# Where the expert weights are split into high and low parts: GpSimd, or ScalarE and VectorE

## The chip, the core and the metric

One core of a Trainium2 chip runs the whole program. Time is the device time of one execution in microseconds (us). Five engines have an instruction queue each and run it in order: TensorE (PE: matmuls; PEld: its weight loads), VectorE (DVE), ScalarE (ACT), GpSimd (POOL) and SyncE (SP), which here only issues DMAs.

## The reference

```python
def reference(**kwargs):
    ...
    attn_out = _attn_ref(**attn_kwargs)      # 2 x 8 heads, 768 tokens, 64 wide, masked by LSH buckets
    x = attn_out.transpose(0, 2, 1, 3).reshape(1536, 512)
    x = ((x @ w1) * (x @ w2)) @ w3 @ w_out                      # 512 -> 1024 -> 1024 -> 512
    p = domain_probs / (domain_probs.sum(-1, keepdims=True) + 1e-09)
    for e in range(4):                                          # the experts
        out += p[:, e:e + 1] * (np.maximum(x @ w1_e, 0.0) @ w2_e)   # 512 -> 1024 -> 512
```

All is fp32. The change touches the second and third stage, the products with `w3 @ w_out` and the four experts.

## The kernel before

**Arithmetic.** A product of fp32 matrices is made of three matmuls in fp32r: high x high, high x low, low x high. So each operand is split: the high part is a copy into an fp32r tile (`hi_of` on ACT, `pool_hi` on GpSimd), the low part is the value less its high part (`lo_of` on DVE, `pool_lo` on GpSimd).

**Stages after attention.** (1) `A` and `B` are the products with w1 and w2; their element product g is kept. (2) `W` i (i = 0 to 7) is one eighth of w3 @ w_out, 24 matmuls each, and its result is split by ACT and DVE. (3) `H` blk, ff multiplies g by it: three blocks of 512 tokens with eight steps of 12 matmuls. The steps of block 0 are mixed among the W, those of block 1 and 2 follow. (4) For each expert, `M` and `N` are the first layer, by Strassen's seven products over two token blocks (M, 512 columns) and the third block (N, 256 columns), for four column pairs fp of the weight; `O` are the steps of the second layer, 24 matmuls per fp for block 0 (mixed among M and N), and 96 each for blocks 1 and 2 behind them. One fp has 7 x 6 matmuls M, 7 x 6 matmuls N and 24 matmuls O.

**Weights of the experts.** `conv_full` loads a quarter of a first layer (`load_u`, into buffer `wraw` 0) or of a second layer (`load_o`, `wraw` 1) by two DMAs of 256 KB and splits it on GpSimd: a first-layer quarter as two tiles of 128x256 (`dh`, and `dc`/`dd` for the low parts), a second-layer quarter as one tile of 128x1024 (`dh`, `dd`). For the first layer, DVE also makes five sums of its parts for Strassen's products (`z`, into `zf`, all reading `wraw`), ACT makes their high parts (`zh`, 128x1024 and 128x256) and DVE their low parts (`zl`); the split sums lie in one tile, which the next sums may take only when the N products 1, 2, 5, 7 and 6 have read it. `wraw` is loaded anew when its splits and its sums are done. The weights of stages 1 and 2 go through `conv64`, ten steps on ACT and DVE per half tile, which this change leaves as they are.

**Sums of the input.** At the end of H's block 1, DVE makes sums of the result (`xs`, L899), which ACT and DVE split (`yh`, `xd`); at the end of block 2, the sums `ys` (L875) and their splits `yi`, `yd`, which N reads. N's four results are combined by DVE (`ya1` to `y22`) in tiles called kept(2, ff), until block 2's O reads them.

**Order.** `op` records each step with an engine, a planned duration, the steps it waits for and a priority. `emit_all` plays the program by these durations and the delays in `LAT` (a DMA: its duration and 1900 ns more), takes on each engine the ready step of least priority value, and writes the instructions in the order that comes out. Planned durations decide the order alone; on the chip every engine goes through that order and waits where an operand is late.

Of the kernel before, what the change touches and what calls it, by code (L numbers as in the profile page):

```python
# [71 lines left out]
def tile_lsh_attention_moe(ctx, tc, qk, v, projc, w1, w2, w3T, w_out, dp, e1, e2, out):  # L72
# [107 lines left out]
    def conv64(n, dst, half, src):  # L180
        r = raws[n % NRAW]

        def hi_():
            return slots[dst][:, 0, half * 512:(half + 1) * 512]

        def lo_():
            return slots[dst][:, 1, half * 512:(half + 1) * 512]

        ri = r.bitcast(I32)
        lw, hw = (ri.rearrange("p (a b) -> p a b", b=2)[:, :, i] for i in range(2))  # L190
        c, t = cbuf[:, n % NCB, 0], cbuf[:, n % NCB, 1]
        beside = n < NBESIDE
        side, sdur, seng, minus = ("POOL", 1290, nc.gpsimd, pool_lo) if beside else ("DVE", 620, nc.vector, lo_of)
        slow = (400, 700) if beside else (335, 602)
        return [
            ("SP", 2700, [("cd", n - NRAW), ("c2", n - NRAW)], "cl",
             lambda: nc.sync.dma_start(out=ri.rearrange("p (a b) -> p a b", a=src.shape[1]), in_=src)),
            ("ACT", 570, [("cl", n), ("cq", n - NCB)], "ca",
             lambda: nc.scalar.activation(out=f(c), in_=f(hw), func=AF.Abs)),
            ("DVE", slow[0], [("ca", n)], "c0",  # L200
             lambda: nc.vector.tensor_scalar(out=f(c), in0=f(c), scalar1=EXP_LO, scalar2=EXP_HI, op0=ALU.max, op1=ALU.min)),
            ("DVE", slow[0], [("c0", n)], "c1",
             lambda: nc.vector.tensor_scalar(out=t, in0=c, scalar1=3, scalar2=0x3FFFFFFF, op0=ALU.logical_shift_left,
                                             op1=ALU.bitwise_and)),
            ("DVE", slow[1], [("c1", n)], "c2",
             lambda: nc.vector.scalar_tensor_tensor(out=c, in0=hw, scalar=-0x40000000, in1=t, op0=ALU.bitwise_and,
                                                    op1=ALU.bitwise_or)),
            ("DVE", slow[0], [("c2", n)], "c3",
             lambda: nc.vector.tensor_scalar(out=t, in0=c, scalar1=-0x800000, scalar2=None, op0=ALU.bitwise_and)),
            ("ACT", 520, [("c2", n)], "ch",  # L210
             lambda: nc.scalar.activation(out=hi_(), in_=f(c), func=AF.Copy)),
            (side, sdur, [("ch", n)], "cp", lambda: minus(lo_(), f(c), hi_())),
            ("DVE", slow[1], [("c3", n)], "cd",
             lambda: nc.vector.scalar_tensor_tensor(out=f(t), in0=lw.bitcast(U32), scalar=2.0 ** -52, in1=f(t),
                                                    op0=ALU.mult, op1=ALU.mult)),
            (side, sdur, [("cp", n), ("cd", n)], "cq",
             lambda: seng.tensor_tensor(out=lo_(), in0=f(lo_()), in1=f(t), op=ALU.add)),
        ]
# [425 lines left out]
    nh = [0]  # L644
# [88 lines left out]
    ZB = L_[0]  # L733
    raw_free = [[(k, 2 * (4 + 4 + 4 + KF) - NRAW + i) for k in ("cd", "c2")] for i in range(NRAW)]

    def conv_full(name, dst, fn, src, fp, after, raw, z_after=None):
        T = clock[0]
        r = raws[raw]
# [6 lines left out]
                out=r[:, half * 512:(half + 1) * 512].rearrange("p (a b) -> p a b", a=s_.shape[1]), in_=s_),  # L745
               raw_free[raw], T - 1.5 * P)
        if z_after is None:
            op(("dh", name), "POOL", 1170, lambda: pool_hi(slots[dst][:, 0], r), got + after, T)
            op(("dd", name), "POOL", 2420, lambda: pool_lo(slots[dst][:, 1], r, slots[dst][:, 0]), [("dh", name)], T)
        else:  # L750
            rq = r.rearrange("p (j k f c) -> p j f k c", j=2, k=2, f=2)
            for i in range(2):
                key = ("dd" if i else "dc", name)
                op(("dh", name, i), "POOL", 310, lambda i=i: pool_hi(a_at(fp, i)[:, 0], rq[:, i, i]), got + after, T)
                op(key, "POOL", 640, lambda i=i: pool_lo(a_at(fp, i)[:, 1], rq[:, i, i], a_at(fp, i)[:, 0]), [("dh", name, i)], T)
        raw_free[raw] = [("dd", name), ("dc", name)]
        if z_after is None:
            return
# [1 line left out]
        for m, (sa, a, b) in enumerate(((1.0, (0, 0), (1, 1)), (-1.0, (0, 1), (1, 1)), (-1.0, (0, 0), (1, 0)),  # L760
                                        (1.0, (1, 0), (1, 1)), (1.0, (0, 1), (0, 0)))):
            def go(m=m, sa=sa, a=a, b=b):
                nc.vector.scalar_tensor_tensor(out=zs_t[1][:, m], in0=q[:, a[0], a[1]], scalar=sa,
                                               in1=q[:, b[0], b[1]], op0=ALU.mult,
                                               op1=ALU.add if m == 0 else ALU.subtract)

            op(("z", name, m), "DVE", 340, go, got + z_after, T)
            raw_free[raw].append(("z", name, m))
        for i, (ms, dur) in enumerate(((slice(0, 4), 1080), (slice(4, 5), 270))):
            src = lambda ms=ms: zs_t[1][:, ms]  # L770
            op(("zh", name, i), "ACT", dur, lambda i=i, src=src: hi_of(zz(i)[:, 0], src()),
# [69 lines left out]
    for blk in range(NB):  # L841
        hb = u_ps if blk % 2 else o_ps
        for ff in range(KF):
# [61 lines left out]
    x_in = [("xd", m, k) for m in range(1, 8) for k in range(2)]  # L905
    y_in = [("yd", m) for m in range(1, 8)]
    u_in = [k for r in freed[1] for k in r]
    load_u(0, 1, [("W", KF - 1)], [("N", 0, 0, m) for m in (1, 2, 5, 6, 7)])
    last_o[0] = [("hl", NB - 1, d) for d in range(KM)]

    def kept(blk, ff):
        return G[ff // 4][:, ff % 4] if blk == 1 else G[2][:, ff] if ff < 4 else f(cbuf.rearrange(
            "p a b c -> p (a b) c"))[:, ff - 4]

    def relu_hi(n, key, after, m):
        op(key, "ACT", 480, lambda: nc.scalar.activation(out=hl_t[n % 2][:, 0], in_=m_t[m], func=AF.Relu), after, clock[0])  # L916
# [29 lines left out]
    def put_down(e, blk, ff, n, ready, ps, free_):  # L946
# [1 line left out]
        order[blk].append(ff)  # L948
        down(("O", e, blk, ff), n, lambda d, a: hl_t[n % 2][:, a, d * 128:(d + 1) * 128],
             lambda d, b: slots[OB[ff // 2]][:, b, (ff % 2) * 512:(ff % 2 + 1) * 512],  # L950
             i == 0, i == KF - 1, ready + [("dd", ("O", e, ff // 2))] + (free_ if i == 0 else [("O", e, blk, order[blk][-2])]), ps)

    kept_key = {}
    for e in range(NE):
        order = [[] for _ in range(NB)]
        old = x_in + y_in + [("gl", nh[0] - 1 - k) for k in range(16 if e else 0)]
        for fp in range(4):
            name = ("U", e, fp)

            def w(fp=fp):  # L960
# [146 lines left out]
```

## Time and profile before

| | us |
|---|---|
| median of 3 runs (994.08, 994.24, 997.37) | 994.24 |
| the profiled execution | 993.28 |
| its span, first to last instruction | 991.5 |

The span begins with attention (to about 264 us), then stage 1 (to 373), W with block 0 of H (to 439), the other blocks of H (to about 485, where the first M stands among them) and the experts, of which the second begins at 616.05, the third at 740.08 and the fourth at 864.14. The TensorE clock was granted at 0.999 of full speed on average. Busy time says only that an engine has an instruction under way; where the order of the queues decides, one reads what each engine waited for and which instruction took longer than its like.

### The profile page before, as it was taken

The page shows a single profiled execution, that of the slowest core. Times are in us where ns is not written, and L with a number is a line of the kernel's source. Part 1 is how long each engine was busy: PE and PEld are TensorE (multiplying, and loading weights), DVE is VectorE, ACT ScalarE, POOL GpSimd, SP SyncE. Part 2 cuts the span into 40 slices and gives each one's busy share as a digit, 9 for nine tenths or more (in the row PEclk, how much of TensorE's full clock was granted, in tenths as well). Part 3 has the DMA queues.
Part 4 walks back from the last instruction along what each step waited for, and adds up shares of the span by engine and source line. Part 5 has one row for each costly group of instructions (what it writes and reads, how often), then busy time and mean ns, then how long its engine had stood idle before and what let it go on. Part 6 is the DMA issues. An engine that isn't in the chain of part 4 may idle for free.

```text
span 991.5 us, 14182 instructions
## 1 busy us (share of the span) xinstructions
PE 970.0 (98%) x5227; PEld 832.6 (84%) x5227; DVE 718.1 (72%) x1341; ACT 428.6 (43%) x784; POOL 280.9 (28%) x319
## 2 busy tenths in 40 slices
PE   8999999999999999999889999999999999999998
PEld 7989899889788888877778888888888888888886
DVE  7999999999599975965886644766446664466543
ACT  6999999988443322443422222222222222222221
POOL 6978877665000000021410014200142001420000
PEclk9999999999999999999999999999999999999999
DMA  6645434221033331310200001100011000100011
GB/s 170 192 111 132 116 94 125 71 73 44 1 128 128 107 106 44 127 64 1 86 22 22 29 15 55 53 22 28 16 55 52 22 26 16 57 30 22 2 54 74
DMA packets 40901, 64.18 MB, mean 65 GB/s; under 512 B 5400, under 2 KB 23832, under 8 KB 40832
## 3 DMA queue, kind: packets, MB, share of 16 engines
q1 hardware_dynamic: 40688, 63.27, 21.4%
q8 instruction: 41, 0.67, 0.3%
q14 instruction: 28, 0.23, 0.1%
q10 hardware_dynamic: 144, 0.01, 0.0%
HBM read 47.22 MB, written 3.15 MB: 51 GB/s over the span
## 4 chain that ended last, share of the span: by engine, by line
PE 81%; DVE 12%; ACT 4%; issue 2%; POOL 0%; DVEq 0%; ACTq 0%; POOLq 0%
PE u_ps L149 49%; PE o_ps L149 19%; PE s_ps L149 5%; PE pv_ps L149 3%; PE t_ps L462 3%; DVE et L470 3%; DVE e L428 2%; PE t_ps L149 1%; ACT e L431 1%; ACT et L468 1%; DVE hl L919 1%; DVE xa L489 1%; PE t_ps L517 1%; DVE slot L158 1%; DVE hl L158 1%
## 5 line engine op out<-in xcount | busy, mean ns | idle before, releaser
L149 PE MATMUL o_ps<-slotl,hl 128*128 128x512 f32 x768 | 178.8, 390 | 0.4 <-DVE hl L919 0.2
L149 PEld LDWEIGHTS o_ps<-slotl,hl 128*128 128x128 f32 x768 | 142.9, 188 | 30.5 <-DVE hl L919 1.7
L149 PE MATMUL u_ps<-xh,slotl 128*128 128x512 f32 (+1 forms) x672 | 137.5, 359 | 0.7 <-DVE g L924 0.7
L149 PEld LDWEIGHTS u_ps<-xh,slotl 128*128 128x128 f32 x672 | 114.3, 189 | 19.6 <-DVE g L924 0.9
L161 POOL TENSOR_SCALAR slot<-wraw 128x256 fp32r<-128x256 f32 x32 | 14.9, 468 | 404.8 <-DMA wraw<-in_e 224.4
L924 DVE TENSOR_TENSOR m<-m,u_ps 128x512 f32<-128x512 f32 x96 | 63.1, 684 | 74.9 <-PE u_ps L149 73.2
L149 PE MATMUL u_ps<-xh,slot 128*128 128x512 f32 (+1 forms) x576 | 116.1, 354 | 1.2 <-DVE xh L158 1.2
L149 PEld LDWEIGHTS u_ps<-xh,slot 128*128 128x128 f32 x576 | 97.1, 189 | 18.0 <-DVE xh L158 1.6
L470 DVE TENSOR_TENSOR et<-t_ps,et 128x512 fp32r<-128x512 f32 x144 | 96.5, 683 | 4.0 <-ACT et L468 3.2
L431 ACT ACTIVATE e<-e,sm 128x768 f32<-128x768 f32 x96 | 89.3, 931 | 9.4 <-DVE e L428 9.0
L428 DVE TENSOR_SCALAR_CACHE_REDUCE e<-s_ps 128x768 f32<-128x768 f32 x96 | 90.2, 943 | 0.9 <-PE s_ps L149 0.9
L149 PE MATMUL pv_ps<-et,vv 128*128 128x256 f32 x576 | 89.1, 292 | 0.7 <-DVE xa L489 0.4
L462 PE MATMUL t_ps<-ident,e 128*128 128x128 f32 x576 | 84.2, 274 | 3.6 <-DVE et L470 3.0
L149 PE MATMUL u_ps<-slotl,hl 128*128 128x512 f32 x384 | 87.7, 389 | 0.0
L468 ACT ACTIVATE et<-t_ps 128x512 fp32r<-128x512 f32 x144 | 82.8, 591 | 10.4 <-PE t_ps L462 5.7
L149 PEld LDWEIGHTS u_ps<-slotl,hl 128*128 128x128 f32 x384 | 72.1, 188 | 15.0
L149 PEld LDWEIGHTS pv_ps<-et,vv 128*128 128x128 f32 x576 | 74.5, 190 | 2.6 <-DVE xa L489 1.0
L462 PEld LDWEIGHTS t_ps<-ident,e 128*128 128x128 f32 x576 | 65.7, 140 | 11.8 <-DVE et L470 3.9
L441 POOL TENSOR_SCALAR e<-e,sm 128x768 f32<-128x768 f32 x72 | 68.5, 960 | 16.9 <-DVE sm L446 15.7
L919 DVE SCALAR_TENSOR_TENSOR hl<-gl,hl 128x512 fp32r<-128x512 f32 x32 | 23.7, 742 | 54.3 <-ACT hl L1051 46.2
L161 POOL TENSOR_SCALAR slotl<-wraw 128x1024 fp32r<-128x1024 f32 x16 | 17.0, 1062 | 156.6 <-PE o_ps L149 125.2
L916 ACT ACTIVATE hl<-m 128x512 fp32r<-128x512 f32 x32 | 20.3, 633 | 92.1 <-DVE m L924 92.1
(154 smaller groups left out, 1634.4 us busy)
## 6 DMA issues: line engine op xcount, KB each, us to landing
wraw<-in_e SPq DMA_DIRECT2D x64, 256.0 KB
wraw<-in_w SPq DMA_DIRECT2D x16, 512.0 KB
wraw<-in_w3T SPq DMA_DIRECT2D x16, 512.0 KB
r<-in_qk SPq DMA_DIRECT2D x15, 384.0 KB
wraw<-in_w_out SPq DMA_DIRECT2D x8, 512.0 KB
rv<-in_v SPq DMA_DIRECT2D x16, 192.0 KB
out<-xa SPq DMA_DIRECT2D x12, 256.0 KB
ka<-hh SPq DMA_DIRECT2D x15, 192.0 KB
```

Of the source, the lines that this page charges most:

```text
L149: nc.tensor.matmul(out=o, lhsT=l, rhs=r, start=start, stop=stop)
L158: nc.vector.tensor_tensor(out=dst, in0=ps, in1=f(hi), op=ALU.subtract)
L161: nc.gpsimd.tensor_scalar(out=o, in0=i, scalar1=1.0, scalar2=1.0, op0=ALU.mult, op1=ALU.mult)
L428: op(("mx", u, t), "DVE", 873, lambda ps=ps, m=m, e=e: nc.vector.tensor_scalar(out=e, in0=ps[:, 0:S], scalar1=THR, scalar2=None, op0=ALU.m ...
L431: op(("ex", u, t), "ACT", 921, lambda e=e, m=m, rs=rs: nc.scalar.activation(out=e, in_=e, func=AF.Exp, scale=-1.0, bias=m, accum_out=rs), ...
L441: return "POOL", 872, lambda: nc.gpsimd.tensor_scalar(out=e, in0=e, scalar1=r[:, t:t + 1], scalar2=1.0, op0=ALU.mult, op1=ALU.mult)
L462: nc.tensor.transpose(out=ps[:, k, t * 128:(t + 1) * 128], in_=e_t[2 * (u % ER) + t][:, kt * 128:(kt + 1) * 128], identity=ident)
L468: op(("hi", n), "ACT", 480, lambda ps=ps, et=et: nc.scalar.activation(out=et[:, 0], in_=ps, func=AF.Copy), [("T", u, j), ("pv", n - NET)], Tj)
L470: op(("lo", n), "DVE", 602, lambda ps=ps, et=et: nc.vector.tensor_tensor(out=et[:, 1], in0=ps, in1=f(et[:, 0]), op=ALU.subtract), [("hi", ...
L916: op(key, "ACT", 480, lambda: nc.scalar.activation(out=hl_t[n % 2][:, 0], in_=m_t[m], func=AF.Relu), after, clock[0])
L919: op(key, "DVE", 602, lambda: nc.vector.scalar_tensor_tensor(out=hl_t[n % 2][:, 1], in0=src(), scalar=0.0, in1=f(hl_t[n % 2][:, 0]), op0=A ...
L924: nc.vector.tensor_tensor(out=out, in0=a, in1=b, op=o)
```

## The change

- The splits of the experts' weights leave GpSimd. High parts are ACT copies, low parts DVE subtractions; a second-layer quarter is split as two halves of 512 columns, each waiting for its own DMA and each with a key of its own (`dc`, `dd`).
- The five sums z of the next first-layer quarter no longer wait in the plan for the N products that read the tile of split sums, but for the split (`zl`) of the former sums, as `zf` is free then. The splits zh still wait for these N products.
- The tiles kept(2, ff) change places: ff 0 to 3 in `cbuf`, ff 4 to 7 in `G[2]` (before, the other way round), and the results of fp 0 and 1 no longer wait for all splits `yd`.
- The first expert's second quarter of the first layer, and the quarters 1 to 3 of its second layer, wait for later steps than before.
- The planned duration of a `conv64` load behind attention is 1460 ns and no longer 2700 ns. Nothing that is issued changes by it, but the planner starts those conversions earlier.

```diff
-        slow = (400, 700) if beside else (335, 602)
+        slow = (400, 700, 2700) if beside else (335, 602, 1460)
         return [
-            ("SP", 2700, [("cd", n - NRAW), ("c2", n - NRAW)], "cl",
+            ("SP", slow[2], [("cd", n - NRAW), ("c2", n - NRAW)], "cl",
...
+    zlast = [None]
+
     def conv_full(name, dst, fn, src, fp, after, raw, z_after=None):
...
         if z_after is None:
-            op(("dh", name), "POOL", 1170, lambda: pool_hi(slots[dst][:, 0], r), got + after, T)
-            op(("dd", name), "POOL", 2420, lambda: pool_lo(slots[dst][:, 1], r, slots[dst][:, 0]), [("dh", name)], T)
+            for h in range(2):
+                key, w = ("dd" if h else "dc", name), slice(h * 512, (h + 1) * 512)
+                op(("dh", name, h), "ACT", 520, lambda w=w: hi_of(slots[dst][:, 0, w], r[:, w]), got[h:h + 1] + after, T)
+                op(key, "DVE", 602, lambda w=w: lo_of(slots[dst][:, 1, w], r[:, w], slots[dst][:, 0, w]), [("dh", name, h)], T)
...
-                op(("dh", name, i), "POOL", 310, lambda i=i: pool_hi(a_at(fp, i)[:, 0], rq[:, i, i]), got + after, T)
-                op(key, "POOL", 640, lambda i=i: pool_lo(a_at(fp, i)[:, 1], rq[:, i, i], a_at(fp, i)[:, 0]), [("dh", name, i)], T)
+                op(("dh", name, i), "ACT", 270, lambda i=i: hi_of(a_at(fp, i)[:, 0], rq[:, i, i]), got + after, T)
+                op(key, "DVE", 331, lambda i=i: lo_of(a_at(fp, i)[:, 1], rq[:, i, i], a_at(fp, i)[:, 0]), [("dh", name, i)], T)
...
-            op(("z", name, m), "DVE", 340, go, got + z_after, T)
+            op(("z", name, m), "DVE", 340, go, got + [("zl", zlast[0], i) for i in range(2)], T)
             raw_free[raw].append(("z", name, m))
+        zlast[0] = name
...
-                load_o(0, min((ff + 1) // 2, 3), [("H", blk, ff - 1), ("H", blk, ff)])
+                load_o(0, min((ff + 1) // 2, 3), [("H", blk, ff - 1), ("H", blk, ff), ("N", 0, 0, 6)])
...
-    load_u(0, 1, [("W", KF - 1)], [("N", 0, 0, m) for m in (1, 2, 5, 6, 7)])
+    load_u(0, 1, [("W", KF - 1), ("H", NB - 1, KF - 1)], [("N", 0, 0, m) for m in (1, 2, 5, 6, 7)])
...
-        return G[ff // 4][:, ff % 4] if blk == 1 else G[2][:, ff] if ff < 4 else f(cbuf.rearrange(
-            "p a b c -> p (a b) c"))[:, ff - 4]
+        return G[ff // 4][:, ff % 4] if blk == 1 else G[2][:, ff - 4] if ff > 3 else f(cbuf.rearrange(
+            "p a b c -> p (a b) c"))[:, ff]
...
-        old = x_in + y_in + [("gl", nh[0] - 1 - k) for k in range(16 if e else 0)]
+        was = x_in + [("gl", nh[0] - 1 - k) for k in range(16 if e else 0)]
         for fp in range(4):
+            old = was + (y_in if fp > 1 else [])
```

What it does to the queues, at three places. First TensorE where W ends: `u_ps3 <- ..., slot3` is the last one, W 7 (24 matmuls), and `o_ps <- hl, slotl3` are the steps 6 (hl0) and 7 (hl1) of H's block 0.

```order
+L149 MATMUL u_ps3_3043<-slotl4_3026,slot3_65 128x512 x6
+L149 MATMUL u_ps3_3043<-slotl5_3027,slot3_65 128x512 x6
+L149 MATMUL u_ps3_3043<-slot0_62,slot3_65 128x512 x6
+L149 MATMUL u_ps3_3043<-slot1_63,slot3_65 128x512 x6
 L149 MATMUL o_ps0_3044<-hl0_3030,slotl3_3025 128x512 x3
 L149 MATMUL o_ps1_3045<-hl0_3030,slotl3_3025 128x512 x3
 L149 MATMUL o_ps2_3046<-hl0_3030,slotl3_3025 128x512 x3
 L149 MATMUL o_ps3_3047<-hl0_3030,slotl3_3025 128x512 x3
-L149 MATMUL u_ps3_3043<-slotl4_3026,slot3_65 128x512 x6
-L149 MATMUL u_ps3_3043<-slotl5_3027,slot3_65 128x512 x6
-L149 MATMUL u_ps3_3043<-slot0_62,slot3_65 128x512 x6
-L149 MATMUL u_ps3_3043<-slot1_63,slot3_65 128x512 x6
```

W 7 now stands ahead of step 6, and two steps, not one, lie between it and block 1. Of the earlier W, 3, 4 and 5 also begin one step sooner, 6 as before.

Then DVE from the last sums of block 1's end to the first combination of the first expert's products, before:

```order
L158 TENSOR_TENSOR slot1_63<-cbuf_70,slot1_63 128x512 x2
L158 TENSOR_TENSOR hl0_3030<-gl1_3029,hl0_3030 128x512
L763 SCALAR_TENSOR_TENSOR zf_3037<-wraw0_68 128x256 x5
L158 TENSOR_TENSOR hl1_3031<-gl1_3029,hl1_3031 128x512
L158 TENSOR_TENSOR slotl0_3022<-zf_3037,slotl0_3022 128x1024
L158 TENSOR_TENSOR zs_3032<-zf_3037,zs_3032 128x256
L875 TENSOR_TENSOR gl0_3028<-gl1_3029 128x512 x2
L924 TENSOR_TENSOR m2_3035<-m0_3033,u_ps2_3042 128x512
```

and now:

```order
L158 TENSOR_TENSOR slot1_63<-cbuf_70,slot1_63 128x512 x2
L158 TENSOR_TENSOR hl0_3030<-gl1_3029,hl0_3030 128x512
L158 TENSOR_TENSOR slotl0_3022<-zf_3037,slotl0_3022 128x1024
L158 TENSOR_TENSOR zs_3032<-zf_3037,zs_3032 128x256
L158 TENSOR_TENSOR hl1_3031<-gl1_3029,hl1_3031 128x512
L767 SCALAR_TENSOR_TENSOR zf_3037<-wraw0_68 128x256 x5
L880 TENSOR_TENSOR gl0_3028<-gl1_3029 128x512
L158 TENSOR_TENSOR slot2_64<-wraw0_68,slot2_64 128x256 x2
L929 TENSOR_TENSOR m2_3035<-m0_3033,u_ps2_3042 128x512
```

The first sums `zf` are gone from here (they now stand at the end of W, ahead of block 1), those shown are of the second quarter, and the low parts `slot2` of that quarter are new on DVE.

Last ACT in block 2 of the first expert's second layer, the relus `hl` of ff 0 to 5, before:

```order
L1051 ACTIVATE hl0_3030<-gl1_3029 128x512
L1051 ACTIVATE hl1_3031<-gl1_3029 128x512
L1051 ACTIVATE hl0_3030<-gl1_3029 128x512
L1051 ACTIVATE hl1_3031<-gl1_3029 128x512
L1051 ACTIVATE hl0_3030<-cbuf_70 128x512
L1051 ACTIVATE hl1_3031<-cbuf_70 128x512
```

and now, with the next expert's first two quarters of the second layer (`slotl5` and `slotl1`, from `wraw1`) and a product M's result (`m0`) among them:

```order
L1057 ACTIVATE hl0_3030<-cbuf_70 128x512
L1057 ACTIVATE hl1_3031<-cbuf_70 128x512
L1057 ACTIVATE hl0_3030<-cbuf_70 128x512
L155 ACTIVATE slotl5_3027<-wraw1_69 128x512 x2
L1057 ACTIVATE hl1_3031<-cbuf_70 128x512
L1057 ACTIVATE hl0_3030<-gl1_3029 128x512
L155 ACTIVATE m0_3033<-u_ps0_3040 128x512
L155 ACTIVATE slotl1_3023<-wraw1_69 128x512 x2
L1057 ACTIVATE hl1_3031<-gl1_3029 128x512
```

The relu of ff 3 (hl1) waits behind the two copies, that of ff 5 behind the next two; on TensorE, a product M stands ahead of the steps of ff 3, 5 and 7 there. GpSimd's queue loses its 64 instructions on `wraw`, and no arithmetic is left on it behind attention.

## Rows read from the trace of the kernel before

**Rows 1.** The page's first part: busy us (share of span) and instructions.
```profile
PE 970.0 (98%) x5227; PEld 832.6 (84%) x5227; DVE 718.1 (72%) x1341; ACT 428.6 (43%) x784; POOL 280.9 (28%) x319
```

**Rows 2.** Busy us by stretch: us, then PE, PEld, DVE, ACT, POOL, clock, DMA.
```profile
520.00:540.00 20.00, 20.00 (x110) 17.41 (x109) 12.62 (x26) 4.59 (x8) 2.20 (x4) 1.00 0.08 27
...
439.40:616.05 176.65, 169.72 (x817) 141.17 (x817) 113.71 (x185) 54.75 (x94) 34.33 (x32) 1.00 0.09 30
616.05:740.08 124.03, 123.90 (x626) 105.67 (x625) 73.77 (x129) 28.19 (x48) 23.13 (x25) 1.00 0.11 35
```

**Rows 3.** The chain that ended last, by time: start us, us, what.
```profile
429.93 5.45 PE u_ps L149 x24
...
436.05 3.32 PE o_ps L149 x12
...
607.98 2.75 DVE hl L919
...
616.05 14.55 PE u_ps L149 x84
630.61 5.47 PE o_ps L149 x24
...
696.13 21.76 PE u_ps L149 x96
```

**Rows 4.** Waits between 455 and 620 us: total us, times, longest.
```profile
PE o_ps L149 <- DVE hl L158: 4.0, 3, 2.6
```

**Rows 5.** Instructions by time, 465 to 479 us: start us, us, engine, what.
```profile
467.01 1.06 POOL L161 TENSOR_SCALAR slotl<-wraw 128x1024 fp32r<-128x1024 f32 x1 [30.75 <-PE o_ps L149]
467.23 4.16 DVE L158 TENSOR_TENSOR slot<-m,slot 128x512 fp32r<-128x512 f32 x2
...
468.15 2.69 POOL L164 TENSOR_TENSOR slotl<-wraw,slotl 128x1024 fp32r<-128x1024 f32 x1
...
472.65 5.73 PE L149 MATMUL o_ps<-hl,slotl 128*128 128x512 f32 x24 [2.56 <-DVE hl L158]
...
474.31 1.28 DVE L158 TENSOR_TENSOR slotl<-cbuf,slotl 128x512 fp32r<-128x512 f32 x2
...
476.59 2.39 POOL L164 TENSOR_TENSOR slotl<-wraw,slotl 128x1024 fp32r<-128x1024 f32 x1
476.72 2.81 DVE L158 TENSOR_TENSOR hl<-gl,hl 128x512 fp32r<-128x512 f32 x1
```

**Rows 6.** TensorE by time in the first expert's first products, 500 to 516 us.
```profile
502.28 0.98 PE L149 MATMUL u_ps<-slot,slotl 128*128 128x256 f32 x6 [1.36 <-ACT gl L155]
503.93 0.98 PE L149 MATMUL u_ps<-xh,slotl 128*128 128x256 f32 x6 [0.67 <-DVE g L924]
...
513.70 0.73 PE L149 MATMUL u_ps<-slot,slotl 128*128 128x512 f32 x2 [0.32 <-ACT slotl L155]
514.96 1.20 PE L149 MATMUL u_ps<-slot,slotl 128*128 128x512 f32 x4 [0.53 <-DVE slotl L158]
```

**Rows 7.** DVE groups by shape: count | busy us, mean ns | idle us <- releasers.
```profile
L763 DVE SCALAR_TENSOR_TENSOR zf<-wraw 128x256 f32<-128x256 f32 x80 | 28.2, 419 | 0.0
L158 DVE TENSOR_TENSOR slotl<-zf,slotl 128x1024 fp32r<-128x1024 f32 x16 | 19.6, 1225 | 10.4 <-ACT slotl L155 10.4
...
L158 DVE TENSOR_TENSOR slot<-cbuf,slot 128x512 fp32r<-128x512 f32 x18 | 12.2, 683 | 0.0
...
L158 DVE TENSOR_TENSOR zs<-zf,zs 128x256 fp32r<-128x256 f32 x16 | 6.9, 431 | 0.0
```

**Rows 8.** The same for ACT.
```profile
L211 ACT ACTIVATE slot<-cbuf 128x512 fp32r<-128x512 f32 x24 | 15.1, 629 | 23.2 <-DVE cbuf L206 23.2
...
L155 ACT ACTIVATE zs<-zf 128x256 fp32r<-128x256 f32 x16 | 6.4, 399 | 0.0
```

**Rows 9.** GpSimd by time: split of a second-layer quarter, idle before it.
```profile
606.64 1.04 POOL L161 TENSOR_SCALAR slotl<-wraw 128x1024 fp32r<-128x1024 f32 x1 [3.36 <-DMA wraw<-in_e]
```

**Rows 10.** DVE alone, where W and H's block 0 are mixed.
```profile
386.00:427.00 41.00, 39.78 (x75) 1.00 0.36 116
```

More of the change, by code (lines that the diff above doesn't have):

```diff
@@ L950, in put_down @@
              lambda d, b: slots[OB[ff // 2]][:, b, (ff % 2) * 512:(ff % 2 + 1) * 512],
-             i == 0, i == KF - 1, ready + [("dd", ("O", e, ff // 2))] + (free_ if i == 0 else [("O", e, blk, order[blk][-2])]), ps)
+             i == 0, i == KF - 1, ready + [(x, ("O", e, ff // 2)) for x in ("dc", "dd")] + (free_ if i == 0 else [("O", e, blk, order[blk][-2])]), ps)
     kept_key = {}
@@ L1017, in tile_lsh_attention_moe @@
                 n, got = mul(m, lhs, have_u, "N", by, W)
-                op(("uf", n), "ACT", 270, lambda n=n, dst=dst: hi_of(dst(), u_ps[n % 4][:, 0:256]), got + old + y_in, clock[0])
+                op(("uf", n), "ACT", 270, lambda n=n, dst=dst: hi_of(dst(), u_ps[n % 4][:, 0:256]), got + old, clock[0])
                 keys[key(f"y{m}")] = keys[("uf", n)]
             n, got = mul(1, lambda: z(0), have_z, "N", by, W)
-            mix("ya1", C11, C21, n, ALU.add, got + old + y_in + [key("y4")], W)
-            mix("yb1", C22, C12, n, ALU.add, got + old + y_in + [key("y3"), key("ya1")], W)
+            mix("ya1", C11, C21, n, ALU.add, got + old + [key("y4")], W)
+            mix("yb1", C22, C12, n, ALU.add, got + old + [key("y3"), key("ya1")], W)
             n, got = mul(2, lambda: z(1), have_z, "N", by, W)
```

## Prediction

> **What bounds the kernel now.** I read the page's busy shares first: TensorE is busy for 98% of the span [rows 1], so whatever the change does to other engines counts only where TensorE stands still. Then the chain of waits, for the pace of undisturbed stretches: 96 matmuls of 512 columns take 21.76 us, so one takes 0.2267; one fp of an expert takes 14.55 + 5.47 = 20.02; an expert at that pace takes 4 x 20.02 + 2 x 21.76 = 123.60 [rows 3]. Against this pace I set three stretches.
>
> A: from the end of W 7 (429.93 + 5.45 = 435.38) to the end of the last step of H's block 0 (436.05 + 3.32 = 439.37) are 3.99 us with one step of 12 matmuls in them, 2.72: 1.27 us lost [rows 3].
> B: from there to the second expert's first product at 616.05 are 176.68 us, the work is 21.76 for each of H's blocks 1 and 2 and 123.60 for the first expert, together 167.12: 9.56 us lost [rows 3]. The row of that stretch shows 6.9 us without a matmul; the rest is matmuls that are under way longer [rows 2].
> C: the second expert takes 124.03 [rows 2], the third 864.14 - 740.08 = 124.06 by the table of stages: 0.43 and 0.46 lost.
>
> Sum: 11.72 us. No more can be won here, since attention and stage 1 keep the order of their matmuls.
>
> Last the instructions by time, for what is late in B. At 467.23 DVE's two low parts take 4.16 us; the next pair of that kind takes 1.28. GpSimd splits a second-layer quarter just then (467.01 to 470.84). At 476.72 one low part takes 2.81 us beside GpSimd's next subtraction, where its like is a mean of 0.683 [rows 5, 7]. Both times a step of block 2 waits for the low part behind: 2.56 us once [rows 5], 4.0 in three waits [rows 4]. The excess, 2.88 and 2.13, is DVE held while GpSimd works on `wraw`. The chain has another at 607.98, 2.75 us, and that is stretch C's loss too [rows 3]. Later in B, TensorE waits 1.36 and 0.67 for banks and operands that the late sums hold up, then 0.32 + 0.53 for the split sums of z [rows 6].
>
> **The change part by part.**
>
> *GpSimd's splits go.* With them goes what held DVE: by the excess above 5.0 us of DVE time in B ahead of the first expert. What comes: per quarter of the first layer two ACT copies (0.399, bounded by the row of that shape) and two DVE subtractions (0.431), per quarter of the second two copies (0.629) and two subtractions (0.683) [rows 7, 8]. Per expert that is 4 x (0.80 + 1.26) = 8.2 us for ACT and 4 x (0.86 + 1.37) = 8.9 for DVE. In the second expert's stretch ACT is busy 28.2 and DVE 73.8 of 124 [rows 2], so 36 and 83: neither becomes the bound as a whole. What counts is where they stand.
>
> *End of W.* W 7 stands one step earlier. It starts at 429.93 - 2.72 = 427.21 and ends at 432.66; the two steps behind it end at 438.10, if the split of W 7's result (ACT 0.63, DVE 0.68 [rows 7, 8]) is there by 435.38, which leaves over a microsecond. Gain: stretch A's 1.27. This needs the w3 tiles earlier. From W 1's end at 383.7 (counted back from 429.93 by 5.44 and 2.72 a piece) plus 1.3 for two ACT copies (a result's and the tile's), 75 DVE instructions stand up to the last part of W 7's tile; in that stretch 75 took 41.0 us now, DVE busy nearly throughout [rows 10]. So the tile is done at about 426 to 428, and W 7 first reads its second half's low part with its 15th matmul, at 430.4. Bounds: 75 at the 0.683 of the longest kind would be 51.2, 5.7 us late; with no wait nothing is lost. I take the row's pace, nothing. The ACT copies of the first two quarters (0.80 + 1.26) follow the last W and end before step 7 does, so block 1's first operand, behind them, is in time.
>
> *Block 2 of H.* The sums and splits stand on DVE in the same order as now, less the five z (they moved to the end of W). Without the holds each low part is there before its step; I leave 0.6 us for the first steps, which come straight behind the block's sums (one short wait of rows 4 is of that kind).
>
> *First expert, fp 0 and 1.* Here DVE has its new work and the sums ys at once. By counting its queue with the durations of rows 7, three waits remain. The first product of fp 1 waits 0.3 for a bank. Its third product needs zl, 1.225 us on DVE, and the subtractions of a second-layer quarter (1.37) stand ahead of it: TensorE waits 0.55, where it now waits 0.85 [rows 6]. In fp 1, five z and the next quarter's subtractions stand ahead of the combinations that free a bank: 0.6. Together 1.45. From fp 2 on, a stretch of 20 us in which DVE was busy for 12.62 [rows 2] gets 0.86 + 1.37 more, 14.9 of the 20.02 that an fp takes, and the z stand behind all that frees a bank.
>
> *Blocks 2 of the experts' second layers.* ACT's two copies of a quarter and DVE's two subtractions now stand ahead of the relu of ff 3, 5 and 7: 1.26 + 0.63 on ACT and 0.68 on DVE behind, 2.7 with their gaps, while a step takes 2.72. But the new order has a product M (1.36) between each such step and the one before, so 4.08 us cover it, and C's 0.89 is won. If that cover failed, the cost would be a fraction of a microsecond, nine times.
>
> *Plan alone.* kept(2, ff) change places with tiles of the same shape: no cost; the earlier results no longer wait for yd, which the count above uses. The later loads: each wraw is loaded two steps or more ahead of its split. From the last read of a quarter to the next one's landing are 3.36 us [rows 9].
>
> **Sum.** A 1.27 + B (9.56 - 0.6 - 1.45 = 7.51) + C 0.89 = 9.67. The profiled execution took 993.28 (span 991.5 and 1.8 around it), so 983.6; the median of the runs lies 0.96 above it: 984.6. I add 0.9, an estimate, for two waits of the size of the three above that a count by hand has missed: 985.5. No edit of TensorE's work is in it.
>
> A rule speaks against it. In the Trainium skill, Perfetto Trace Analysis (Optimizing Scalar/DVE Operations) says that GPSIMD and DVE share a read port, so that moving work between the two might not help. For the low parts that is what this change does; by the rule alone only the copies that go to ACT would be won. The rows say: GpSimd's copy and subtraction held DVE for 2.88 at 467, and DVE's own two halves take 1.37 at another place of its queue, behind the last W. So I take it as a rival and not as the forecast.
>
> **Rivals.**
>
> *DVE is as late by its own work.* Then the holds' part of the loss stays: 2.56 and the remaining 1.2 of rows 4's long waits, 1.36 + 0.67 of rows 6, C's 0.89, together 6.7; gain 3.0, so 991.3. For it: 8.9 us more DVE work per expert, and the sums ys meet the second quarter's split. Against: the new DVE work in block 2 of H is nothing at all.
>
> *The w3 tiles come late.* DVE is busy for 39.78 of 41 us there [rows 10], and the plan now reckons a load at 1460 + 1900 ns, so ACT may stand in its queue for a landing, and with it what DVE needs. At 5.7 late, A's gain goes with it: about 990. Against: nothing is added to that stretch, and the first tile now begins before W 1's result, not behind it.
>
> *The queues are held by loads: slower.* So far only GpSimd waited for the experts' loads, and nobody for GpSimd. Now ACT's copies stand ahead of relus. Place: three quarters in block 2 of each of three experts, and three in the first expert's fp 0 to 2, twelve holds. A load is issued when DVE's last subtraction is done, 2.1 us behind the release of the tile; 3.36 on, it has landed, at 5.5, and the copy has to wait until 6.8 anyway for the next step (2.72 + 1.36 + 2.72). Margin 1.3. From a landing of 4.7 on the holds cost, from 5.5 on (12 x 0.8) the whole gain is gone; at 5.7, 996.6. Against it: the landing measured, 3.36 [rows 9].
>
> **How the numbers follow.** Forecast 0.70, its own range 982.5 (all 11.72 won) to 988.5 (three times the waits left); late tiles 0.12 (986 to 991.5); DVE late by itself 0.11; held queues 0.07. The range 982.5 to 990.5 leaves out most of the last two. A change of 0.5% (5.0 us) is about what can be told from none. Faster by more, below 989.3: the forecast, half of the late tiles and a little of the next, 0.78; slower 0.07; the same 0.15.
>
> **What would show it.** Right: no DVE instruction of 512 elements above 0.8 us after 430; the step after W 7 starting within 0.1 us of it; block 2 of H with under 1 us of waits; experts 2 and 3 at 123.6 to 123.8. Wrong: TensorE waiting for `slot3` or `slotl3` parts between 390 and 432, or in fp 0 and 1 more than 2 us for DVE; ACT's copies from wraw released by a DMA in block 2, and TensorE behind them.

## The result, and the profile after

The changed kernel takes 983.55 us (median of four runs, 983.32 to 985.26), the kernel before 994.28 beside it: a ratio of 0.9889, 95% interval 0.9866 to 0.9911. The forecast was 985.5 with a range of 982.5 to 990.5. The profiled execution took 983.52, with a span of 981.7 where before had 991.5: 9.8 us less.

The page's first part answers to [rows 1]:

```profile
PE 967.0 (99%) x5227; PEld 832.5 (85%) x5227; DVE 721.7 (74%) x1405; ACT 456.9 (47%) x848; POOL 184.9 (19%) x223
```

GpSimd lost 96 instructions (not 64, as the section on the change has it) and 96 us, ACT got 28 us more. DVE got only 3.6 more, although 32 subtractions of 512 elements and 32 of 256 came: what was held before got shorter. (Added up by their durations, the other DVE instructions took 20 us less; the rest is that neighbours overlap, and the busy time counts an overlap once.) The relu parts made from `cbuf` had a mean of 1194 ns before; among DVE's groups by shape of the changed kernel (columns as in [rows 7]) stand

```profile
L158 DVE TENSOR_TENSOR slotl<-wraw,slotl 128x512 fp32r<-128x512 f32 x32 | 21.9, 689 | 23.0 <-ACT slotl L155 23.0
...
L158 DVE TENSOR_TENSOR slot<-wraw,slot 128x256 fp32r<-128x256 f32 x32 | 13.2, 419 | 0.0
...
L924 DVE SCALAR_TENSOR_TENSOR hl<-cbuf,hl 128x512 fp32r<-128x512 f32 x16 | 11.1, 691 | 15.8 <-PE u_ps L149 8.1 <-ACT hl L1057 7.7
```

No DVE instruction of 512 elements lasts longer than 0.752 us after 430, as the prediction asked. In the kernel before, 16 of the 325 there lasted longer than 0.9 us, and each of the 16 overlaps a GpSimd instruction on a quarter of 1024 columns.

The busy times by stretch, as in [rows 2], cut where TensorE passes from one stage to the next. Stretches in order: stage 1; W with H's block 0; H's block 1 to the first expert's second layer, block 1; then from one expert's block 1 to the next one's, three times. First the kernel before:

```profile
263.91:372.64 108.73, 108.73 (x479) 90.03 (x480) 99.31 (x182) 40.07 (x68) 0.00 (x0) 1.00 0.33 107
372.64:439.21 66.57, 65.88 (x289) 53.91 (x288) 48.82 (x87) 22.24 (x37) 6.81 (x6) 1.00 0.27 87
439.21:571.98 132.77, 125.94 (x626) 105.23 (x624) 93.80 (x161) 45.27 (x79) 22.77 (x24) 1.00 0.10 32
571.98:695.97 123.99, 123.89 (x625) 105.67 (x624) 73.68 (x129) 28.18 (x48) 23.27 (x25) 1.00 0.11 35
```

and the changed one:

```profile
264.46:373.15 108.69, 108.69 (x479) 90.01 (x480) 96.77 (x182) 39.23 (x68) 0.00 (x0) 1.00 0.33 107
373.15:438.43 65.28, 65.28 (x289) 54.05 (x288) 50.18 (x96) 24.02 (x41) 0.00 (x0) 1.00 0.29 91
438.43:563.43 125.00, 124.59 (x625) 105.53 (x624) 92.22 (x177) 51.97 (x96) 0.00 (x0) 1.00 0.10 33
563.43:687.05 123.62, 123.62 (x625) 105.73 (x624) 76.35 (x145) 35.41 (x65) 0.00 (x0) 1.00 0.12 35
```

Call the four "stage 1", "A", "B" and "experts". A went from 66.57 to 65.28 (1.29 won), B from 132.77 to 125.00 (7.77), the experts from 123.99, 124.03 and 124.06 to 123.62 each (1.22): 10.28. Stage 1 is the same; it began 0.55 later (264.46 for 263.91), since attention, in which nothing was changed, took that much longer in this execution. Over all runs below that start lies between 263.9 and 266.2, so they are compared by stretches and not by spans. A stretch with the same order comes out the same each time: A is 65.28 or 65.29 in ten kernels and 66.53 to 66.57 in the other four.

TensorE by time in the changed kernel, at the end of W and in the first expert, answers to [rows 3, 5, 6]:

```profile
430.27 2.88 PE L149 MATMUL u_ps<-slot,slot 128*128 128x512 f32 x12
432.99 5.60 PE L149 MATMUL o_ps<-hl,slotl 128*128 128x512 f32 x24
438.43 22.02 PE L149 MATMUL u_ps<-hl,slotl 128*128 128x512 f32 x96
460.29 3.11 PE L149 MATMUL o_ps<-hl,slotl 128*128 128x512 f32 x13
463.59 16.41 PE L149 MATMUL o_ps<-hl,slotl 128*128 128x512 f32 x71 [0.20 <-DVE hl L158]
...
506.09 1.20 PE L149 MATMUL u_ps<-slot,slotl 128*128 128x512 f32 x4 [0.16 <-DVE slotl L158]
```

The two steps behind W 7 stand back to back with it, and of the waits in [rows 4, 6] only 0.20 and 0.16 are left. DVE in the stretch of [rows 5]:

```profile
466.46 1.29 DVE L158 TENSOR_TENSOR slot<-m,slot 128x512 fp32r<-128x512 f32 x2
...
475.32 0.69 DVE L158 TENSOR_TENSOR hl<-gl,hl 128x512 fp32r<-128x512 f32 x1 [0.36 <-ACT hl L155]
```

The pair that took 4.16 takes 1.29, and the low parts 0.69.

### The profile page after: what moved, and what is told of

The parts are those of the page before. It is cut to its first block, busy times and chain, and to the rows that moved or that the text cites. A ratio compares the mean times of both kernels' runs of the same rounds, so it can differ in the third digit from the quotient of the medians.

```text
span 981.7 us, 14246 instructions
## 1 busy us (share of the span) xinstructions
PE 967.0 (99%) x5227; PEld 832.5 (85%) x5227; DVE 721.7 (74%) x1405; ACT 456.9 (47%) x848; POOL 184.9 (19%) x223
## 4 chain that ended last, share of the span: by engine, by line
PE 83%; DVE 10%; ACT 4%; issue 2%; POOL 1%; DMA 1%; SPq 0%; DVEq 0%; POOLq 0%; ACTq 0%
PE u_ps L149 49%; PE o_ps L149 21%; PE s_ps L149 4%; PE t_ps L462 3%; PE pv_ps L149 3%; DVE et L470 3%; DVE e L428 2%; PE t_ps L149 2%; ACT et L468 1%; ACT e L431 1%; DMA r<-in_qk 1%; DVE xa L489 1%; ACT pvs L487 0%; DVE slotl L158 0%; ACT e L440 0%
## 5 line engine op out<-in xcount | busy, mean ns | idle before, releaser
L149 PE MATMUL s_ps<-ka,hh 128*128 128x512 f32 x192 | 53.3, 358 | 2.6 <-DVE e L428 2.1
L155 ACT ACTIVATE m<-u_ps 128x512 f32<-128x512 f32 x32 | 19.2, 599 | 76.4 <-issue 54.9
```

What stands on the lines that cost most here:

```text
L149: nc.tensor.matmul(out=o, lhsT=l, rhs=r, start=start, stop=stop)
L155: nc.scalar.activation(out=dst, in_=ps, func=AF.Copy)
```

## The experiments

Two theories stood against each other. Theory H (not to be taken for stage H): the gain is that GpSimd no longer holds DVE, as the prediction says. Theory P: the gain is the new order. All kernels are timed against the kernel before on the same chip. Each row of the table is worked out from the starts in that kernel's trace; "experts" are the three periods. The intervals of runs 2, 4 to 7 and 12 overlap that of the changed kernel, so these are told from it by their stretches, one trace each.

| kernel | median us | ratio (95%) | A | B | experts |
|---|---|---|---|---|---|
| before | 994.28 to 995.38 | 1 | 66.57 | 132.77 | 123.99, 124.03, 124.06 |
| changed | 983.55 | 0.9889 (0.9866-0.9911) | 65.28 | 125.00 | 123.62 x3 |
| 1 splits alone | 989.11 | 0.9946 (0.9933-0.9958) | 66.55 | 129.76 | 123.62 x3 |
| 2 splits back | 984.57 | 0.9896 (0.9881-0.9911) | 65.28 | 124.35 | 124.37, 124.06, 124.10 |
| 3 late loads alone | 989.20 | 0.9938 (0.9925-0.9952) | 66.53 | 127.79 | 124.24, 124.02, 124.10 |
| 4 loads at 2700 | 984.44 | 0.9897 (0.9883-0.9910) | 66.55 | 124.99 | 123.61, 123.62, 123.62 |
| 5 early loads | 984.23 | 0.9890 (0.9875-0.9906) | 65.28 | 125.49 | 123.62 x3 |
| 6 z as before | 986.26 | 0.9912 (0.9897-0.9927) | 65.29 | 127.03 | 123.62 x3 |
| 7 kept as before | 985.36 | 0.9901 (0.9884-0.9919) | 65.28 | 126.42 | 123.62 x3 |
| 8 idle subtractions | 1000.23 | 1.0055 (1.0043-1.0068) | 65.28 | 142.98 | 123.62 x3 |
| 9 idle copies | 988.21 | 0.9939 (0.9927-0.9950) | 65.28 | 129.88 | 123.94, 123.62, 123.62 |
| 10 subtractions twice | 989.77 | 0.9957 (0.9946-0.9969) | 65.28 | 130.02 | 124.19, 124.17, 124.16 |
| 11 loads twice | 992.31 | 0.9979 (0.9971-0.9988) | 65.28 | 130.14 | 124.54, 124.78, 124.59 |
| 12 first expert on GpSimd | 983.03 | 0.9884 (0.9869-0.9898) | 65.28 | 124.40 | 123.62 x3 |

**1. Splits alone.** The two hunks of `conv_full` that move the splits, put into the kernel before, and `put_down` waiting for `dc` as well; nothing else is edited. The planner makes other queues of it all the same: those of DVE and ACT differ in B, that of TensorE from the first expert's block 2 on.

> The kernel before, with the experts' splits on ScalarE and VectorE and every other line as it was. Theory H (GpSimd's work on wraw holds VectorE): the holds go with the splits, so TensorE's waits in H's block 2 (4.0 us) and the 0.4 us of each of the first three experts come back, some 5 to 7 us, less 1 to 2 for VectorE's own new work in the first fp: 987 to 990. Theory P (the new order is what wins): the old order gets 8.9 us more VectorE work per expert and no gain: 993 to 997.

989.11, as theory H expects. The experts are at 123.62 at once, and B is 3.01 shorter. But 4.76 of the 7.77 are missing: TensorE still waits 1.57, 0.68, 0.32 and 0.53 in the first expert (the rows of [rows 6] were 1.36, 0.67, 0.32, 0.53), and in H's block 2 0.88 for DVE's own new work.

**2. Splits back.** The changed kernel with those two hunks undone:

```diff
-                op(("dh", name, h), "ACT", 520, lambda w=w: hi_of(slots[dst][:, 0, w], r[:, w]), got[h:h + 1] + after, T)
-                op(key, "DVE", 602, lambda w=w: lo_of(slots[dst][:, 1, w], r[:, w], slots[dst][:, 0, w]), [("dh", name, h)], T)
+            op(("dh", name), "POOL", 1170, lambda: pool_hi(slots[dst][:, 0], r), got + after, T)
+            op(("dd", name), "POOL", 2420, lambda: pool_lo(slots[dst][:, 1], r, slots[dst][:, 0]), [("dh", name)], T)
```

> The changed kernel, with the splits on GpSimd again and the rest of the change kept. Theory H: VectorE's subtractions of 512 elements are stretched to 2 us and more again beside GpSimd; only the end of W (1.3 us) and some of the first fp's waits stay won: 989 to 992. Theory P: the order alone holds the gain: 983.5 to 985.5.

984.57, as theory P expects: B is even 0.65 shorter than in the changed kernel, with all splits on GpSimd. What the splits' move still brings within the new plan is the experts: 0.75, 0.44 and 0.48. But the order changes with the engines, in B (TensorE's from 495 on) and in the experts. With the splits on GpSimd, here and in the kernel before, TensorE's 96 matmuls of block 2 stand in one piece; with them on ACT and DVE, in run 1 too, products M stand among them. TensorE by time in the first expert's block 2, in this kernel and then in the changed one:

```profile
585.14 16.94 PE L149 MATMUL o_ps<-slotl,hl 128*128 128x512 f32 x74
602.34 5.28 PE L149 MATMUL o_ps<-slotl,hl 128*128 128x512 f32 x22 [0.27 <-DVE hl L922]
```
```profile
585.19 8.32 PE L149 MATMUL o_ps<-slotl,hl 128*128 128x512 f32 x36
593.35 1.52 PE L149 MATMUL u_ps<-xh,slot 128*128 128x512 f32 x6
```

The experts' loss stands where a held relu part is waited for; whether the missing hold wins it back or the product M that covers it, no run here parts. DVE is held in this kernel too, where it costs little. GpSimd's subtraction and DVE's two relu parts beside it, in this kernel's instructions by time:

```profile
599.35 2.39 POOL L164 TENSOR_TENSOR slotl<-wraw,slotl 128x1024 fp32r<-128x1024 f32 x1
599.38 3.51 DVE L922 SCALAR_TENSOR_TENSOR hl<-gl,hl 128x512 fp32r<-128x512 f32 x2 [2.03 <-ACT hl L1055]
```

Two parts of 0.69 last 3.51, and end 1.15 behind GpSimd's end.

**3. Late loads alone.** The kernel before with one thing of the plan, the later loads of the first expert; the queues of TensorE and DVE are word for word those of before, and GpSimd's first-expert splits alone move.

```diff
-                load_o(0, min((ff + 1) // 2, 3), [("H", blk, ff - 1), ("H", blk, ff)])
+                load_o(0, min((ff + 1) // 2, 3), [("H", blk, ff - 1), ("H", blk, ff), ("N", 0, 0, 6)])
...
-    load_u(0, 1, [("W", KF - 1)], [("N", 0, 0, m) for m in (1, 2, 5, 6, 7)])
+    load_u(0, 1, [("W", KF - 1), ("H", NB - 1, KF - 1)], [("N", 0, 0, m) for m in (1, 2, 5, 6, 7)])
```

> The kernel before, with the later loads of the changed one (the first expert's second quarter of the first layer, its quarters 1 to 3 of the second); GpSimd still splits, and the order of TensorE and VectorE is word for word that of before. Theory H: VectorE is held where GpSimd works, so moving GpSimd's work out of H's block 2 gives back the 2.56 us and most of the 1.2 us of waits there, at some hold in the first two fp: 988 to 991. Theory P (the order of VectorE's queue makes the waits): that order is unchanged, 993.5 to 995.

989.20, as theory H expects. With the same order on TensorE, DVE and also ACT the pair of [rows 5] takes 1.28 and TensorE goes through block 2 with 0.20 of wait (instructions by time, up to 480):

```profile
464.34 15.94 PE L149 MATMUL o_ps<-hl,slotl 128*128 128x512 f32 x69 [0.20 <-DVE hl L158]
...
467.22 1.28 DVE L158 TENSOR_TENSOR slot<-m,slot 128x512 fp32r<-128x512 f32 x2
...
476.06 0.69 DVE L158 TENSOR_TENSOR hl<-gl,hl 128x512 fp32r<-128x512 f32 x1 [0.35 <-ACT hl L155]
```

TensorE alone, in the first expert's fp 0:

```profile
497.07 0.98 PE L149 MATMUL u_ps<-slot,slotl 128*128 128x256 f32 x6 [0.64 <-ACT gl L155]
498.73 0.97 PE L149 MATMUL u_ps<-xh,slotl 128*128 128x256 f32 x6 [0.67 <-DVE g L924]
```

So the hold is shown for B, by taking GpSimd away from DVE in time and not in place. And of the 1.36 of [rows 6] half goes with the hold; the other half and the 0.67 have another cause: run 7.

**4 to 7. The plan's parts, each undone in the changed kernel.** 4 sets `slow` back to 2700 ns; 5 takes back the two lines of run 3; 6 and 7:

```diff
-            op(("z", name, m), "DVE", 340, go, got + [("zl", zlast[0], i) for i in range(2)], T)
+            op(("z", name, m), "DVE", 340, go, got + z_after, T)
```
```diff
-            old = was + (y_in if fp > 1 else [])
+            old = was + y_in
```

(7 also puts the kept tiles back into their places.)

> The changed kernel with the planned duration of a load behind attention at 2700 ns again; W 7 stands behind step 6 of H's block 0 as in the kernel before. If term A is right (1.27 us at the end of W), 984.9, with a loss of 1.3 between the last W's end and the last step of block 0. If that loss was only moved, 983.6.

A is 66.55, 1.27 more, and the 0.69 that step 7 waits for ACT's split of W 7 is there again: term A stands alone, and at its size.

> The changed kernel with the early loads of before; the splits stay on ScalarE and VectorE. Six to eight subtractions (4 to 5 us of VectorE) then stand in H's block 2, where the changed kernel has 5.7 us of VectorE free in 23.6. If own work counts as much as a hold did: a wait of 1 to 3 us there, 984.5 to 986.5. If VectorE has room: 983.4 to 984.

B is 0.49 longer, with one wait of 0.88 in block 2, less than the 1 to 3 expected if own work counted like a hold: DVE has nearly the room.

> The changed kernel with the five sums z waiting in the plan for the N products again. If the order of z counts: the waits of 0.32 and 0.53 us in fp 1 come back, 984 to 984.8; if not, 983.4 to 983.9.

Missed, and by much: B is 2.03 longer. The waits for the split sums of z are 1.63 and 0.53, where before had 0.32 and 0.53 [rows 6]. TensorE by time:

```profile
508.86 0.73 PE L149 MATMUL u_ps<-slot,slotl 128*128 128x512 f32 x2 [1.63 <-ACT slotl L155]
510.12 1.21 PE L149 MATMUL u_ps<-slot,slotl 128*128 128x512 f32 x4 [0.53 <-DVE slotl L158]
```

What ACT's high parts zh (`slotl<-zf`) are late for, here and then in the kernel before:

```profile
504.61 0.75 DVE L767 SCALAR_TENSOR_TENSOR zf<-wraw 128x256 f32<-128x256 f32 x2
505.27 1.29 DVE L158 TENSOR_TENSOR slotl<-wraw,slotl 128x512 fp32r<-128x512 f32 x2
506.48 1.09 DVE L767 SCALAR_TENSOR_TENSOR zf<-wraw 128x256 f32<-128x256 f32 x3
507.76 1.05 ACT L155 ACTIVATE slotl<-zf 128x1024 fp32r<-128x1024 f32 x1
```
```profile
509.02 1.76 DVE L763 SCALAR_TENSOR_TENSOR zf<-wraw 128x256 f32<-128x256 f32 x5
512.60 1.05 ACT L155 ACTIVATE slotl<-zf 128x1024 fp32r<-128x1024 f32 x1
```

TensorE begins the first products of fp 1 at 504.32 here and at 510.47 before, so zh starts 3.44 behind that here and 2.13 before: the 1.31 by which the wait grew. Two of DVE's new subtractions (1.29) stand among the five sums. Without them, an estimate from these rows, the last sum would end 1.96 behind that start, in time for zh at 2.13. By this estimate the added wait in the old order of z is DVE's own new work.

> The changed kernel with the kept tiles in their old places and all results of the first expert waiting for yd again. If that order counts: the waits of 1.36 and 0.67 us for a bank and an operand in fp 0 come back, 985 to 986; if not, 983.4 to 983.9.

B is 1.42 longer, with 0.63 and 0.68 back:

```profile
496.44 0.97 PE L149 MATMUL u_ps<-slot,slotl 128*128 128x256 f32 x6 [0.63 <-ACT gl L155]
498.10 0.98 PE L149 MATMUL u_ps<-xh,slotl 128*128 128x256 f32 x6 [0.68 <-DVE g L929]
```

These are results of fp 0 that wait for `yd`, in the order of the plan alone.

**8 and 9. GpSimd work that nobody waits for.** In the changed kernel, per quarter (8; 9 has `tensor_scalar` with one operand, ten and five of them):

```diff
+        def beside():
+            for i in range(4 if z_after is None else 2):
+                nc.gpsimd.tensor_tensor(out=scr[0], in0=X0(0, i % 4), in1=X0(1, i % 4), op=ALU.subtract)
+
+        op(("pd", name), "POOL", 3500 if z_after is None else 1900, beside, got + after, T)
```

> The changed kernel with GpSimd subtractions that nobody waits for, at the time of each split: four of 128x248 per second-layer quarter, two per first-layer quarter, both operands read from a tile of stage 1 that nothing writes any more, the result put into an unused tile. The order of all other engines is the same. Theory H: VectorE's instructions with two operands in SBUF last 2 to 4 us beside them and TensorE waits for the low parts: 986 to 991. Theory P: what nobody waits for costs nothing: 983.4 to 983.9.

Of this text two things were wrong, and 1000.23 lies far above its range. The tile is still written in H, so the work began at 441.5; and since no instruction of it needs a load, it ran in one piece and not at each split:

```profile
443.47 88.83 POOL L764 TENSOR_TENSOR lpad<-xh 128x248 f32<-128x248 f32 x89 [0.70 <-DVE xh L158]
```

That makes a better test: the queues of TensorE, ACT and DVE are the same, GpSimd is busy in B alone, and B alone is longer, by 17.98 (some of it a granted clock of 0.83 from 500 to 520 and 0.91 from 520 to 540); the experts, without it, are at 123.62. DVE beside it:

```profile
466.63 1.19 DVE L158 TENSOR_TENSOR hl<-xa,hl 128x512 fp32r<-128x512 f32 x1
467.74 0.68 DVE L911 TENSOR_TENSOR m<-u_ps,gl 128x512 f32<-128x512 f32 x1
468.34 1.81 DVE L158 TENSOR_TENSOR slot<-m,slot 128x512 fp32r<-128x512 f32 x2
```

What reads two SBUF tiles is stretched from 0.69 to 1.19, what reads one of its two from PSUM (`u_ps`) stays at 0.68; none of the former lasts longer than 1.21, where 2 to 4 us were expected. No engine waits for GpSimd in it: this is the hold of theory H by itself.

> As the run with GpSimd subtractions that nobody waits for, but copies with one operand: ten of 128x248 per second-layer quarter, five per first-layer quarter; they stand in one run behind stage W again, 240 of them. If each read of GpSimd holds VectorE's instructions with two operands in SBUF as the subtractions did: 995 to 1000. If only GpSimd's instructions with two operands do: 983.4 to 984.5.

Between the two: copies hold as well, but less. B is 4.88 longer, and the same rows read:

```profile
465.37 0.87 DVE L158 TENSOR_TENSOR hl<-xa,hl 128x512 fp32r<-128x512 f32 x1
466.16 0.68 DVE L911 TENSOR_TENSOR m<-u_ps,gl 128x512 f32<-128x512 f32 x1
466.76 1.55 DVE L158 TENSOR_TENSOR slot<-m,slot 128x512 fp32r<-128x512 f32 x2
```

**10. Subtractions twice**, for the first rival:

```diff
-                op(key, "DVE", 602, lambda w=w: lo_of(slots[dst][:, 1, w], r[:, w], slots[dst][:, 0, w]), [("dh", name, h)], T)
+                op(key, "DVE", 602, lambda w=w: [lo_of(slots[dst][:, 1, w], r[:, w], slots[dst][:, 0, w]) for _ in range(2)], [("dh", name, h)], T)
```

(and the same for the first layer's.)

> The changed kernel with each of VectorE's new subtractions done twice (the second writes the same values), the order unchanged otherwise: 8.9 us more VectorE work per expert. If VectorE is late by its own work: it is busy 18 and 18.7 of 20 us in the first expert's first two fp, so these lose 2 to 4 us, and the other fp and experts (14 of 20) nothing: 985.5 to 988. If VectorE is near the bound everywhere: each expert's 8.9 us shows in part, above 992.

Missed: 989.77. The first place is as expected (one wait of 2.12 in fp 1, 0.60 at the start of H's block 1), but the wait is dearer than its length, and each expert loses 0.55 too (one wait of 0.30 of it is seen). Busy times by stretch, with the granted clock in the last column but two:

```profile
502.00:510.10 8.10, 6.04 (x35) 4.84 (x33) 7.96 (x19) 3.86 (x7) 0.00 (x0) 1.00 0.12 34
510.10:518.00 7.90, 7.81 (x27) 6.34 (x28) 7.83 (x17) 1.90 (x3) 0.00 (x0) 0.78 0.49 138
```

In TensorE's rows twelve matmuls of 512 columns then take 4.49 instead of 2.88: 1.6 more behind the 2.1.

**11. Loads twice**, for the rival that ends slower: each second-layer load issued twice into the same buffer.

> The changed kernel with each load of a second-layer quarter issued twice, one behind the other into the same buffer, so that its landing comes 3 to 5 us later and ScalarE's copies stand in the queue for it. If the margin is the 1.3 us counted before: twelve holds of 0.8 us and more, 990 to 995. If the copies have room, 983.4 to 984.5.

992.31, 8.8 above the changed kernel (by stretches 5.14 in B, where the granted clock was 0.81 from 511 to 520, and 3.05 in the experts), as the rival says, but in another place. ACT waits 39.9 us for landings in 18 waits between 500 and 870; in block 2 of the experts this costs TensorE nothing. Its waits (3.31, and 0.65 to 0.92 in each later expert) stand where the first layer's next products need a bank. Instructions by time in the first expert's fp 1:

```profile
514.08 0.63 ACT L155 ACTIVATE slotl<-wraw 128x512 fp32r<-128x512 f32 x1 [3.51 <-DMA wraw<-in_e]
...
514.74 0.69 DVE L158 TENSOR_TENSOR slotl<-wraw,slotl 128x512 fp32r<-128x512 f32 x1 [2.85 <-ACT slotl L155]
515.35 0.68 DVE L929 TENSOR_TENSOR m<-m,u_ps 128x512 f32<-128x512 f32 x1
...
516.08 1.19 PE L149 MATMUL u_ps<-xh,slot 128*128 128x256 f32 x4 [3.31 <-DVE m L929]
```

The copy waits for the DMA, the subtraction for the copy, the combination `m` for its turn behind the subtraction, and TensorE for the bank that it frees. In the changed kernel ACT waits 0.9 us for landings in that whole time, in two waits.

**12. The first expert on GpSimd**, what runs 2 and 3 point to: `conv_full` splits on GpSimd where the weights are the first expert's, on ACT and DVE otherwise.

```diff
-        if z_after is None:
+        if name[1] == 0 and z_after is None:
+            op(("dh", name), "POOL", 1170, lambda: pool_hi(slots[dst][:, 0], r), got + after, T)
+            op(("dd", name), "POOL", 2420, lambda: pool_lo(slots[dst][:, 1], r, slots[dst][:, 0]), [("dh", name)], T)
+        elif z_after is None:
```

(and the like for the first layer.)

> The changed kernel with the first expert's weights alone split on GpSimd, where the late loads put that work beside VectorE instructions that nobody waits for; the other experts' on ScalarE and VectorE. From the stages of the runs so far: up to the first expert's block 1 as with all splits on GpSimd (0.65 us less than in the changed kernel), each later expert 123.62 (0.4 less than with GpSimd): a span 0.6 under the changed kernel's, 983.0. If VectorE is held where it counts: 984 to 985.

983.03, the lowest median of all, and by stretches 0.60 below the changed kernel; but that it is faster is shown by the stretches alone: B is 124.40, as with all splits on GpSimd (124.35), and the experts are at 123.62.

## Why the prediction was right, and where it was not

*A*, 1.27 predicted: 1.29, and 1.27 when undone alone. The w3 tiles were in time, as taken from [rows 10].

*B and C*, 8.40 together: 8.99. The steps left over were counted too high: 0.6 in block 2 was 0.20, the bank wait of 0.3 and the 0.6 behind the sums z did not come, and 0.55 for `zl` was 0.16. So 2.05 was 0.36 in waits (the other 1.04 of what B has above 123.60, the pace of [rows 3], shows as no wait). The 0.9 added for waits missed was not needed; without it the forecast was 984.6. Of the 1.95 by which the forecast was too high most of the rest is the 0.96 from the profiled execution to the median: here the two differ by 0.03. That the profiled execution, 983.6 by the sum, came out at 983.52 is in part luck: 0.61 more was won than the 9.67, and the span's start, up to stage 1, took 0.55 longer.

*The step that failed* is "GpSimd's splits go. With them goes what held DVE": not the hold, which runs 3, 8 and 9 show, but what removes it. The prediction gave B to the engines' change and "Plan alone" no gain of its own beyond the waits for yd. Run 2 wins all of B with the splits on GpSimd, run 1 less than half of it with the old plan; put to run 2, the prediction's own reasoning gave 989 to 992 (theory H). The plan's parts, each measured by itself, are 4.98 for the late loads (run 3), 2.03 for z (run 6) and 1.42 for kept (run 7). Their sum, 8.43, is near run 2's 8.42, but it is no proof: runs 6 and 7 have the splits on ACT and DVE, and what z is worth with the splits on GpSimd was not run. Either remedy takes the hold away in B, so together they count once. Within the new plan the change of engines, with the order it brings, wins the experts' 0.75, 0.44 and 0.48 and costs B 0.65: by stretches 1.02 of the 10.3 won.

The sum came out because the prediction counted waits that would go, whoever let them go; for B the right size with the wrong remedy is luck. z was the part least understood: TensorE's wait for z's splits was to fall by 0.3 (0.85 to 0.55), and 2.03 is what z's order is worth beside the new DVE work (run 6).

*The rivals.* DVE late by its own work had 0.11; run 10 shows how near that was: another 8.9 us per expert, and 6.2 of the 10.7 are gone; and run 6 shows it real in one place, where the new order of z takes it away. Late w3 tiles: nothing of it. Held queues: real when each load is issued twice, through the banks of the first layer and not through block 2; with the loads as they are, nothing.

The rule of the Trainium skill that spoke against the change (Perfetto Trace Analysis, Optimizing Scalar/DVE Operations: moving work between GPSIMD and DVE might not help) is not borne out in the old plan, where the splits' move alone makes B 3.01 shorter (run 1), but it is in the new one: with the late loads, moving the splits off GpSimd makes B 0.65 longer (run 2). The rule speaks of work between those two alone; here the high parts go to ACT. The Trainium skill's page SBUF — State Buffer (Who interferes with whom) says that a DVE instruction with two SBUF inputs contends with a GpSimd instruction that reads SBUF, and that one with at most one SBUF input, outside DVE's 2-port modes, does not. Runs 8 and 9 agree: 1.19 and 0.87 for 0.69, and 0.68 unchanged with an operand in PSUM.

## What to carry to other kernels

An instruction that is held shows as a long one and not as a wait: compare it with its like, then look what GpSimd did in that time. A hold can be removed in place or in time; where the held engine is nearly full, moving the other engine's work by a later load may win as much as taking the work over. Before a gain is given to one edit, undo that edit alone: edits that remove the same wait don't add up.

## What the runs showed of the hardware beyond that

- GpSimd's one-operand copies hold DVE too, by less: 0.87 for 0.69 beside copies, 1.19 beside subtractions (runs 9 and 8).
- Beside GpSimd's long subtractions (128x1024, 2.38 to 2.72 us each, the kernel before) a DVE instruction of 512 elements lasted up to 2.88 us; beside its short ones (128x248, about 1.0 us each, run 8) none with two SBUF operands lasted longer than 1.21.
- A wait of TensorE can cost more than its length. Behind 2.12 us in run 10 the granted clock fell to 0.78 of full speed over 8 us, a mix of the levels 1.2 and 2.4 GHz; in the kernel before it stayed at 1.00 behind the 2.56 us at 472 [rows 5], as this row (columns as in [rows 2]) has it. Which of the waits lower it was not settled here.

```profile
474.00:478.00 4.00, 4.00 (x20) 3.29 (x18) 4.00 (x6) 2.32 (x4) 2.62 (x2) 1.00 0.00 0
```
